# A fused adaLN attention block: the last two x tiles loaded on ScalarE's queue

## The chip, the cores and the metric

The kernel runs on one core of a Trainium2 chip. The metric is the device time of one execution in microseconds, as the median of several runs. Beside it stands one profiled execution of the same kernel, from which all views of the profile come; its span is counted from the first to the last instruction of the program and is a little shorter than the device time.

## The reference

x is 2 x 256 tokens of 1152 features, c is 2 x 1152, all in bfloat16:

```python
B, N, D = (2, 256, 1152)
mod = (_silu(c) @ w_mod).reshape(B, 6, 1, D)
shift_a, scale_a, gate_a, shift_m, scale_m, gate_m = [mod[:, i] for i in range(6)]
h = _layernorm(x, axis=-1) * (1 + scale_a) + shift_a
qkv = h @ wqkv
q, k, v = (qkv[..., :D].copy(), qkv[..., D:2 * D].copy(), qkv[..., 2 * D:].copy())
p = _softmax(jnp.einsum('bqd,bkd->bqk', q, k) * D ** (-0.5), axis=-1)
a = jnp.einsum('bqk,bkd->bqd', p, v) @ wo
return x + gate_a * a
```

Only the first three of the six modulation vectors (shift, scale, gate) reach the output.

## The kernel before, in words

**Tiles.** The 512 tokens are four tiles of 128 (`x_sb[:, t, :]`, 288 KB each, tiles 0 and 1 of the first batch entry, 2 and 3 of the second). The 1152 features are nine blocks of 128 (`KT`). Weights are loaded in pieces: `wS` holds the scale columns of `w_mod`, `wH` the shift columns, `wG` the gate columns, `wK` the key columns of `wqkv`, `wqv` the chunks of the query and value columns, `wO` the output projection. All of them, 21 MB, pass through SyncE's DMA queue in the order in which the code issues them; only c, and one of the last pieces of the output, are issued on ScalarE's queue.

**Order.** Every engine's instructions are recorded by a thin wrapper (`spq` for SyncE, `sca` for ScalarE, `vec`, `ten`, `gps`) and at the end `pin` fixes the order on each engine to the order in the code. A DMA that is issued through `sca` thus stands in ScalarE's instruction stream at the place where the code has it, and what is behind it on ScalarE is issued after it. Since every operation passes through one wrapper, nearly all of them have the same line (L78) in the profile and are told apart by their tiles.

The transfers take eight DMA semaphores in turn, in the order of the code over both queues. Before a transfer is issued, its queue waits until the transfer that had the same semaphore before, eight places earlier, has landed. So at most eight transfers are under way at once.

**The early stage, where the change lies.** The fillers are 13 matmuls on a constant that keep TensorE busy until the first real work. Meanwhile:

- c arrives, `sca.activation(out=e_sb, ... Exp)` and three VectorE steps make silu(c) in `scT_f`; ScalarE spreads it in `silu_rep` to `scT_rep`.
- Tile 1 gets its mean and variance on VectorE (`dve_stats`, `dve_aggr`) and is centred there (`centre`). For tiles 0, 3 and 2 the mean comes from ScalarE: `act_mean(t)` is a copy with row sums and then a small scaling of the sums to the mean. `centre(t)` then subtracts it on VectorE.
- TensorE turns the centred tiles by `turned` (nine 128 x 128 transposes into a PSUM bank `tp`), VectorE copies the first three blocks out of it to `xnT` and ScalarE the rest (`from_psum`).
- TensorE makes the first three blocks of the scale (`scale_A`, into `psS` and `psSA`), VectorE multiplies the turned tile with it (`scaled`, into `hTs`), and TensorE starts the keys (`k_part`, into six accumulators `acc`, and `early_half`, into `psE`), for tiles 0 and 1 together, then tile 3, then tile 2.
- The second third of the scale (`psM`) is made between the transposes of tile 2 and its `k_part`.

The six accumulators take the six PSUM banks of one pool, which held the fillers and the transposes of tiles 0 and 1; an accumulator can only start when the copy out of the bank before it is done. The transposes of tiles 3 and 2 follow each other in one other bank.

ScalarE's order in this stage is: issue of c, exponential, `act_mean(0)`, `silu_rep`, `act_mean(3)`, copy of tile 0's transposes, `act_var(0)`, `act_mean(2)`, copy of tile 3's transposes, copy of `psE`, copy of tile 2's transposes, `act_var(2)`. `act_var` is a square with row sums for the variance. SyncE's order is: x tiles 1, 0, 3, five pieces of `wS`, three pieces of `wK`, x tile 2, the next piece of `wK`, three pieces of `wS`, three of `wK` and so on.

After this stage come the rest of the keys, the queries, the scores, the softmax, the values and the output projection; none of their lines is touched.

```python
def act_mean(t):
    sca.activation(out=xc[:, t, :], in_=x_sb[:, t, :], func=ACT.Copy, accum_out=sums[:, t, 0:1])
    sca.activation(out=mv[:, t, 0:1], in_=sums[:, t, 0:1], func=ACT.Copy, scale=1.0 / D)
```

Of the kernel before, what the change touches and what calls it, by code (L numbers as in the profile page):

```python
# [16 lines left out]
def kernel(  # L17
# [10 lines left out]
    P = 128  # L28
# [17 lines left out]
    x_f = x.rearrange("b n d -> (b n) d")  # L46
# [39 lines left out]
    sca = _Rec(nc.scalar, act_seq)  # L86
    ten = _Rec(nc.tensor, pe_seq)
    spq = _Rec(nc.sync, sp_seq)
# [11 lines left out]
    def tok(b):  # L100
# [5 lines left out]
        out=ident, in_=ident, compare_op=ALU.not_equal, fill=1.0, base=0,  # L106
# [14 lines left out]
        out=pick, in_=pick, compare_op=ALU.is_ge, fill=0.0, base=0,  # L121
# [3 lines left out]
        out=pick, in_=pick, compare_op=ALU.is_ge, fill=0.0, base=NT - 1,  # L125
# [6 lines left out]
    x_sb = act.tile([P, TT, D], BF16)  # L132
# [6 lines left out]
    wS = wmpool.tile([P, KT, D], BF16, tag="wS")  # L139
    wH = wmpool.tile([P, KT, D], BF16, tag="wH")  # L140

    def load_x(t):
        spq.dma_start(out=x_sb[:, t, :], in_=x_f[t * P : (t + 1) * P, :])

    def load_mod(tile_, which, k0, k1, c0, c1):
        spq.dma_start(out=tile_[:, k0:k1, c0:c1], in_=wmod_v[:, k0:k1, which, c0:c1])
# [1 line left out]
    def load_k(k0, k1, c0=0, c1=D):  # L148
        spq.dma_start(out=wK[:, k0:k1, c0:c1], in_=wqkv_v[:, k0:k1, D + c0 : D + c1])

    PAIRS = ((0, 2), (2, 4), (4, 6), (6, 8), (8, 9))
    CA = KA * P
    load_x(1)
    load_x(0)
    load_x(3)
    for k0, k1 in PAIRS:
        load_mod(wS, 1, k0, k1, 0, CA)
    load_k(0, 1, 0, CA)
    load_k(0, 1, CA, WE)
    load_k(1, 2, 0, WE)  # L160
    load_x(2)
    load_k(2, 3, 0, WE)
    CM = KM * P
    for k0 in range(0, KT, 3):
# [20 lines left out]
    fillers(13)  # L185
    e_sb = small.tile([P, 2 * KT], F32, tag="e_sb")
    sca.activation(out=e_sb, in_=cT, func=ACT.Exp, scale=-1.0)
    scT_f = const.tile([P, KT, B], F32)
    scT_rep = const.tile([P, KT, NR // B, B], BF16)

# [10 lines left out]
    def silu_rep():  # L201
        sca.copy(out=scT_rep, in_=scT_f.unsqueeze(2).to_broadcast([P, KT, NR // B, B]))
# [25 lines left out]
# [3 lines that stand above are left out]
# [140 lines left out]
    centre(0)  # L371
    silu_rep()
    act_mean(3)

    def bank(name="tp", n=KT - KA, pool=psum, tag="mm"):
        return pool.tile([P, n, P], BF16, tag=tag, name=name)
# [342 lines left out]
```

## Time and profile before

| what | value |
|---|---|
| median of 3 runs | 97.02 us (96.97 to 97.61) |
| the profiled execution | 97.0 us, span 95.2 us |
| granted TensorE clock | 1.0 |
| TensorE busy | 90.8 us (95%) |
| VectorE busy | 70.6 us (74%) |
| ScalarE busy | 33.5 us (35%) |
| HBM read, written | 19.76 MB, 1.18 MB |
| DMA share in 6.8 to 14.9 us | 1.01, 344 GB/s |

The profile names engines PE (TensorE's matmuls), PEld (its weight loads), DVE (VectorE), ACT (ScalarE), POOL (GpSimd) and SP (SyncE). ACTq and SPq are the instruction queues of ScalarE and SyncE, in which DMAs are issued. A row of a timeline has the start in us, the length, the engine, the operation, the tiles it writes and reads, how many of them were merged, and in brackets how long the engine was idle before it and what released it. The mean length of a matmul is not its cost, because matmuls overlap; in the chain of waits their ends are taken apart.

### The profile page before, as it was taken

The page shows a single profiled execution, that of the slowest core. Times are in us where ns is not written, and L with a number is a line of the kernel's source. Part 1 is how long each engine was busy: PE and PEld are TensorE (multiplying, and loading weights), DVE is VectorE, ACT ScalarE, POOL GpSimd, SP SyncE. Part 2 cuts the span into 40 slices and gives each one's busy share as a digit, 9 for nine tenths or more (in the row PEclk, how much of TensorE's full clock was granted, in tenths as well). Part 3 has the DMA queues.
Part 4 walks back from the last instruction along what each step waited for, and adds up shares of the span by engine and source line. Part 5 has one row for each costly group of instructions (what it writes and reads, how often), then busy time and mean ns, then how long its engine had stood idle before and what let it go on. Part 6 is the DMA issues. An engine that isn't in the chain of part 4 may idle for free.

```text
span 95.2 us, 1731 instructions
## 1 busy us (share of the span) xinstructions
PE 90.8 (95%) x678; PEld 54.6 (57%) x682; DVE 70.6 (74%) x138; ACT 33.5 (35%) x68; POOL 21.4 (22%) x26
## 2 busy tenths in 40 slices
PE   5998999999999999999999999999999999999980
PEld 1338899454436444444458665665668756656670
DVE  0488689134998999999997999990129577998880
ACT  5069867201571935322340455242225400000020
POOL 6600000810000000000000000009999980025000
PEclk9999999999999999999999999999999999999999
DMA  2999999999999999999999802200000000303131
GB/s 76 299 336 337 313 361 384 386 392 405 395 379 399 380 402 410 375 376 361 372 406 410 342 39 55 60 2 0 0 0 0 0 0 7 124 0 124 75 117 56
DMA packets 19015, 21.31 MB, mean 224 GB/s; under 512 B 2752, under 2 KB 13632, under 8 KB 19008
## 3 DMA queue, kind: packets, MB, share of 16 engines
q1 hardware_dynamic: 18592, 21.16, 62.2%
q10 hardware_dynamic: 416, 0.05, 0.4%
q8 instruction: 5, 0.08, 0.3%
q14 instruction: 2, 0.02, 0.0%
HBM read 19.76 MB, written 1.18 MB: 220 GB/s over the span
## 4 chain that ended last, share of the span: by engine, by line
PE 95%; DVE 1%; issue 0%; ACT 0%
PE ps L78 64%; PE acc L78 13%; PE junk_ps L78 6%; PE s_ps L78 4%; PE tp L78 2%; PE psE L78 1%; PE psH L78 1%; PE psL L78 1%; PE psM L78 1%; PE psSA L78 1%; PE psS L78 0%; PE spread_ps L78 0%; DVE hTs L78 0%; ACT o_sb L78 0%; DVE junk_rhs L78 0%
## 5 line engine op out<-in xcount | busy, mean ns | idle before, releaser
L78 POOL PARTITION_ALL_REDUCE gate_bc<-gacc x2 | 13.7, 6887 | 44.8 <-DVE gacc L78 44.8
L78 DVE SCALAR_TENSOR_TENSOR gacc<-wG,scT_f,gacc 128x1152 f32<-128x1152 bf16 x16 | 22.7, 1418 | 0.5
L78 PE MATMUL ps<-wqv,hT 128*128 128x384 bf16 x108 | 17.7, 326 | 0.0
L78 PE MATMUL ps<-hT,wqv 128*128 128x512 bf16 x80 | 17.6, 379 | 0.1
L78 PE MATMUL ps<-wO,attnT 128*128 128x384 bf16 (+1 forms) x108 | 17.0, 319 | 0.0
L78 PEld LDWEIGHTS <-attnT 128*128 128x128 bf16 x126 | 11.4, 98 | 6.3
L78 PEld LDWEIGHTS <-hT 128*128 128x128 bf16 x108 | 10.6, 98 | 6.9
L78 PEld LDWEIGHTS <-wK 128*128 128x128 bf16 x123 | 10.1, 97 | 6.9 <-issue 0.5
L78 PE MATMUL acc<-hTs,wK 128*128 128x128 bf16 (+2 forms) x88 | 13.2, 292 | 0.5 <-DVE hTs L78 0.3
L78 PEld LDWEIGHTS <-wqv 128*128 128x128 bf16 x81 | 7.9, 98 | 9.5
L78 ACT CAST qkT<-ps 128x512 bf16<-128x512 f32 x10 | 5.7, 584 | 10.8 <-PE ps L78 10.8
L78 DVE TENSOR_TENSOR ga<-ps,gate_bc 128x384 f32<-128x384 f32 (+1 forms) x12 | 6.5, 538 | 2.7 <-PE ps L78 2.7
L78 ACT CAST v_sb<-ps 128x384 bf16<-128x384 f32 x10 | 4.7, 477 | 9.8 <-PE ps L78 9.8
L78 DVE TENSOR_TENSOR o_sb<-ga,x_sb 128x384 bf16<-128x384 f32 (+1 forms) x12 | 6.8, 564 | 0.4
L78 PE MATMUL junk_ps<-junk_rhs 128*128 128x512 bf16 x13 | 5.7, 630 | 1.1 <-DVE junk_rhs L78 1.1
L78 DVE TENSOR_TENSOR xnT<-xnT,rstd_bc 128x512 bf16<-128x512 bf16 x9 | 5.5, 684 | 1.6 <-ACT rstd_bc L78 1.6
L78 ACT CAST o_sb<-ps 128x128 bf16<-128x128 f32 (+1 forms) x2 | 0.5, 240 | 17.0 <-PE ps L78 17.0
L78 DVE BATCH_NORM_STATS2 stats<-x_sb 128x6 f32<-128x384 bf16 x6 | 3.1, 552 | 2.7 <-DMA x_sb<-in_x_dram 2.7
L78 PE MATMUL ps<-hTs,wK 128*128 128x512 bf16 x20 | 4.8, 380 | 0.1
L78 DVE CAST attnT<-ps 128x512 bf16<-128x512 f32 (+1 forms) x6 | 3.5, 603 | 1.7 <-PE ps L78 1.7
L78 DVE CAST v_sb<-ps 128x384 bf16<-128x384 f32 x2 | 1.1, 558 | 4.6 <-PE ps L78 4.6
L78 DVE TENSOR_SCALAR hTs<-xnT,s1p 128x256 bf16<-128x256 bf16 (+1 forms) x20 | 4.2, 272 | 0.1
(82 smaller groups left out, 88.0 us busy)
## 6 DMA issues: line engine op xcount, KB each, us to landing
wqv<-in_wqkv_dram SPq DMA_DIRECT2D x5, 864.0 KB, 10.1
wG<-in_w_mod_dram SPq DMA_DIRECT2D x3, 864.0 KB, 9.7
wO<-in_wo_dram SPq DMA_DIRECT2D x3, 864.0 KB, 8.5
wH<-in_w_mod_dram SPq DMA_DIRECT2D x4, 576.0 KB, 7.2
wS<-in_w_mod_dram SPq DMA_DIRECT2D x6, 288.0 KB, 6.4
wK<-in_wqkv_dram SPq DMA_DIRECT2D x6, 288.0 KB, 7.2
x_sb<-in_x_dram SPq DMA_DIRECT2D x4, 288.0 KB, 4.2
wqv<-in_wqkv_dram SPq DMA_DIRECT2D x3, 288.0 KB, 8.4
```

The lines of the kernel that those rows point to most:

```text
L78: r = fn(*a, **k)
```

## The change

`load_x` gets the queue as an argument. The load of x tile 3 moves from the third place of SyncE's queue to ScalarE's queue, behind the exponential of silu, and that of x tile 2 from between two pieces of `wK` on SyncE's queue to ScalarE's queue, behind `act_mean(3)`. The order of everything else stays, on all engines. On ScalarE the two issues are two more instructions; on SyncE there are two fewer.

```diff
-    def load_x(t):
-        spq.dma_start(out=x_sb[:, t, :], in_=x_f[t * P : (t + 1) * P, :])
+    def load_x(t, eng=spq):
+        eng.dma_start(out=x_sb[:, t, :], in_=x_f[t * P : (t + 1) * P, :])
...
     load_x(1)
     load_x(0)
-    load_x(3)
     for k0, k1 in PAIRS:
         load_mod(wS, 1, k0, k1, 0, CA)
     load_k(0, 1, 0, CA)
     load_k(0, 1, CA, WE)
     load_k(1, 2, 0, WE)
-    load_x(2)
     load_k(2, 3, 0, WE)
...
     sca.activation(out=e_sb, in_=cT, func=ACT.Exp, scale=-1.0)
+    load_x(3, sca)
...
     silu_rep()
     act_mean(3)
+    load_x(2, sca)
```

In the semaphores' turn, tile 3 now comes behind the fourth piece of `wS` and tile 2 behind the first of the next three pieces of `wS`. So the second of these three waits for tile 3 to land, and the third of the last three pieces of `wS` for tile 2; tile 2 itself waits for the fourth piece of `wS`.

## The prediction

> **What bounds the kernel now.** I read the page's busy row first, then the chain of waits in order of time, then ScalarE's and VectorE's timelines between 3 and 16 us, then the DMA issues one by one. The busy row and one wait list say how much there is to win at all:
>
> ```profile
> PE 90.8 (95%) x678; PEld 54.6 (57%) x682; DVE 70.6 (74%) x138; ACT 33.5 (35%) x68; POOL 21.4 (22%) x26
> ```
>
> The list of TensorE's own waits between 6 and 26 us has this one line:
>
> ```profile
> PE acc L78 <- DVE hTs L78: 0.3, 1, 0.3
> ```
>
> TensorE is the bound. It starts at 1.11 us on fillers that last to 6.81 whatever is loaded, and from there to 92.5 its work is nearly back to back. Its gaps are 0.33 us ahead of the first K product (9.33), about 0.12 us ahead of the third K step (11.52 to 11.64, where its weight load waits for wK) and some 0.15 us at 14.7 to 14.9. So nothing done to loads can bring more than about 0.6 us, 0.6% of the time. A loss has no such limit: whatever comes late to TensorE before 26 us is added to the end, since no later gap takes it up. The chain of waits shows the last of these places, the x tile 2 part (columns: start, length, what):
>
> ```profile
> 13.69 0.45 PE tp L78 x8
> 14.14 0.71 PE psM L78 x27
> 14.85 0.03 issue
> 14.88 1.17 PE acc L78 x18
> ```
>
> The 1.17 us are `k_part` for tile 2. What it waits for comes from x tile 2 through ScalarE (row sums and mean) and VectorE. ScalarE's timeline (start, length, idle before and its releaser in brackets):
>
> ```profile
> 3.90 0.22 ACT L78 ACTIVATE e_sb<-c_sb 128x18 f32<-128x18 bf16 x1 [1.84 <-DMA c_sb<-in_c_dram]
> ...
> 7.34 1.16 ACT L78 ACTIVATE xc<-x_sb 128x1152 bf16<-128x1152 bf16 x1
> ...
> 8.62 0.20 ACT L78 ACTIVATE mv<-sums 128x1 f32<-128x1 f32 x1
> 8.73 0.78 ACT L78 COPY xnT<-tp 128x768 bf16<-128x768 bf16 x1
> ...
> 10.99 1.16 ACT L78 ACTIVATE xc<-x_sb 128x1152 bf16<-128x1152 bf16 x1 [0.32 <-DMA x_sb<-in_x_dram]
> ...
> 12.28 0.20 ACT L78 ACTIVATE mv<-sums 128x1 f32<-128x1 f32 x1
> ```
>
> The row at 10.99 is the key one: ScalarE already waits 0.32 us there for x tile 2 to land. VectorE goes on from its mean (12.28):
>
> ```profile
> 12.51 0.52 DVE L78 TENSOR_SCALAR xc<-x_sb,mv 128x1152 bf16<-128x1152 bf16 x1
> 12.95 1.02 DVE L78 BATCH_NORM_STATS2 stats<-x_sb 128x6 f32<-128x384 bf16 x2
> 14.18 0.36 DVE L78 COPY xnT<-tp 128x384 bf16<-128x384 bf16 x1 [0.21 <-PE tp L78]
> 14.57 0.58 DVE L78 TENSOR_SCALAR hTs<-xnT,s1p 128x128 bf16<-128x128 bf16 x3
> ```
>
> Centring of tile 2, two statistics of tile 3, the copy of the transposes, the three scalings, then the products at 14.88. This string has one slack, the 0.21 us ahead of the copy. **A microsecond of delay of tile 2 costs TensorE 0.8 us.**
>
> The DMA issues give latencies. In order, with issue times from SyncE's and ScalarE's timelines: x tile 1 (0.79), tile 0 (1.25), tile 3 (1.71), tile 2 (6.85), and c on ScalarE's queue (0.81); the last number is us from issue to landing:
>
> ```profile
> x_sb<-in_x_dram SPq DMA_DIRECT2D x1, 288.0 KB, 2.9
> ...
> x_sb<-in_x_dram SPq DMA_DIRECT2D x1, 288.0 KB, 4.2
> ...
> x_sb<-in_x_dram SPq DMA_DIRECT2D x1, 288.0 KB, 4.6
> ...
> x_sb<-in_x_dram SPq DMA_DIRECT2D x1, 288.0 KB, 4.1
> ...
> c_sb<-in_c_dram ACTq DMA_DIRECT2D x1, 4.5 KB, 3.1
> ```
>
> Tile 1 went into an empty system: 2.9 us. The others stand in SyncE's first-in first-out backlog. From 2 us to 52 us the DMA row of the page is at 9, so whatever is put ahead pushes the rest back.
>
> **The change, part by part.** The two loads keep size and shape; they only change queue and time of issue. Nothing is added to VectorE or TensorE.
>
> *Tile 3, issue moved from 1.71 on SyncE to behind the exponential on ScalarE.* The exponential runs at 3.90, released by c, so the issue falls at about 4.0. ScalarE's issue of c lasted 0.46 us, the nearest row; here it ends at 4.5 while ScalarE waits for tile 0 until 5.46, so it costs nothing. Landing: 4.0 plus 2.9 to 3.1 (tile 1, and c on this queue) is 6.9 to 7.1; with 4.6 (tile 3's own latency in the backlog) 8.6. Its user, the row sums at 7.34, is held until 7.34 by the scT_rep copy in any case. I take 7.1: free. At 8.6 the row sums would start 1.3 us late, and the ScalarE copy of tile 0's transposes (8.73 to 9.51) with them; that copy frees the bank of the sixth accumulator, which TensorE takes at 9.87, so 1.3 + 0.36 of issue less the 0.36 of cover is 1.3 us of stall.
>
> *What tile 3's removal does on SyncE.* The issues behind it move up by 0.46 us until the fifth wS transfer, which waits for tile 1 to land; the next ones wait for older landings too, because the built program takes eight DMA semaphores in turn. The first four wS transfers may land up to 0.85 us earlier (288 KB at the 344 GB/s of the 6.8 to 14.9 us window), but tile 3 is then put among them, and with the DMA engines full the fifth wS lands after the same bytes as before, at 8.7 (issue 4.16, 4.5 us). Bounds: 0 to 0.33 us won at the first K product, minus what follows next. I take 0.
>
> *ScalarE's issue of tile 2.* It stands behind tile 3's mean, so it can't go before that is dispatched; the next instruction started at 8.73, so issue at 8.73 instead of 6.85: 1.9 us later. It holds ScalarE's queue for 0.36 us (the final output's issue) to 0.46 (c): the copy of tile 0 now starts at 9.1 to 9.2, ends at 9.9 to 10.0, and the sixth accumulator stalls TensorE by 0.0 to 0.15 us. That is absorbed by the 0.12 ahead of the third K step, provided its wK (issue 7.38, 4.2 us, 11.6) comes earlier, which it does: tile 2 no longer stands ahead of it on SyncE. ScalarE, free for tile 2's row sums at 10.67 until now (the read of tile 0's square sums ends there), is then ready at 11.05 to 11.15, so 10.99 can't be beaten.
>
> *Tile 2's landing,* the term that decides. It is not behind SyncE's backlog but shares the DMA engines with it. From below, 2.9 us (tile 1, empty system): landing 11.6. From above, 4.1 us (its own old latency): 12.8. Nearest in queue and load is c, 3.1 us, though only 4.5 KB; a full tile takes a little longer, so I take 3.2: landing 11.9 instead of 10.97, row sums 0.94 us later.
>
> The sum: 0.94 of delay less 0.21 of VectorE slack is 0.73 us at tile 2's products. The other ways to that point are no later: the transposes of tile 2 need the mean of tile 2 and ScalarE's copy of tile 3 (12.38 to 13.05, now to 14.0) and would end near 14.7, ahead of the two statistics at 14.9. Behind it TensorE is back to back, so 0.73 reaches the end. Nothing else is won there: the 0.12 and 0.15 us gaps lie ahead of the same wait. The profiled execution took 97.0 us (span 95.2 and 1.8 around it; the median shown is 97.02): 97.0 + 0.7 = **97.7 us**. With 2.9 us of latency it is 0.43, 97.4; if the landing were no later than ScalarE is ready (11.05), about 0, 97.0.
>
> By the Trainium skill (DMA: Bandwidth & Descriptors, Issuing engines are not separate DMA queues) loads from several engines run on the same 16 DMA engines and interleave, and only issue time is saved. No row here shows a big load on ScalarE's queue beside the backlog; the rule speaks against a shorter latency and is the first rival's argument.
>
> **The rivals.**
>
> *Tile 2 wins no latency on the other queue.* The engines are full, so it takes the 4.1 us it took before: landing 8.73 + 4.1 = 12.8, row sums 1.87 us later, less 0.21 is 1.66: 98.7 us. For it: DMA at 9 in every slice. Against it: the 4.1 us were spent mostly behind SyncE's earlier transfers, which a load on another queue need not await. It decides from a latency of 3.45 us on, where the loss passes 1%, 0.97 us.
>
> *Both loads are served in order of arrival over both queues,* so the new queue passes nothing. Tile 3 lands near 8.4, since the four wS of the backlog go ahead; tile 2 is then issued at 9.8 and lands like the wK rows issued then, some 5 us later, near 15: 15.0 - 10.99 - 0.21 = 3.8 us, 100.8 us. For it: c, only 4.5 KB, landed at 3.9, after tile 1's 288 KB at 3.7. Against it: c was issued just after tile 1 anyway, so nothing tells the two orders apart.
>
> The Trainium skill (the same page, Queues, rings and completion order) has each DMA engine go round between the queues it has work for, a packet at a time, which speaks against this rival; no row here decides it.
>
> *The early loads win, and tile 2 lands in time.* With tile 3 and tile 2 out of SyncE's way the fifth wS and the third wK come earlier, and tile 2 needs only 2.3 us because its queue is empty. Then up to 0.33 + 0.12 + 0.15 = 0.6 us is won: 96.4 us. Against it: even tile 1 took 2.9 us in an empty system, and 10.99 can't be beaten on ScalarE; so most of these gaps would remain, at best about 96.9.
>
> **How the numbers follow.** A measurement of this kernel tells about 1% from no change. My forecast (latency 2.9 to 3.4 us, 97.4 to 98.0) has 0.47, tile 2 in time or a gain within 1% 0.10, the first rival (3.45 us to 4.6 us, 98.0 to 99.2) 0.31, order of arrival 0.08, a gain over 1% 0.04, as the gaps do not add up to it. So faster 0.04, same 0.57, slower 0.39. The range is 96.9 to 99.0: it takes in the forecast, the tile that is just in time, and most of the first rival.
>
> **What would show it.** After: the issue of tile 3 on ScalarE at 4.0 and of tile 2 near 8.7; the row sums of tile 3 at 7.34 without a wait for DMA; those of tile 2 near 11.9 with an idle time of some 0.9 us put down to x_sb; VectorE's centring of tile 2 at 13.4; TensorE's tile 2 products at 15.6; the rest shifted by 0.7 us. I am wrong if tile 3 is late at 7.34, if tile 2 lands before 11.2 or after 12.3, or if TensorE has the delay made up before the end.

## The result, and the profile after

The changed kernel takes 102.83 us (median of 6, 102.69 to 103.78) against 97.01 us before: a ratio of 1.061, 95% interval 1.057 to 1.065. The forecast was 97.7 us, in a range of 96.9 to 99.0; the loss is 5.8 us instead of 0.7. The profiled execution took 102.78 us, span 100.8 against 95.2. Here and below a median takes in every execution, and a ratio leaves out those that took over 1.5% longer than the fastest of the same kernel.

The chain of waits of the changed kernel, in order of time (start, length, what), no longer runs through TensorE's early work. It runs through the two moved loads:

```profile
3.98 4.56 DMA x_sb<-in_x_dram
...
8.56 1.26 ACT xc L78 x2
...
9.86 5.89 DMA x_sb<-in_x_dram
...
15.77 1.26 ACT xc L78 x2
...
17.89 1.01 PE tp L78 x8
18.90 1.21 PE psM L78 x27
20.11 1.63 PE acc L78 x18
...
98.12 0.21 ACT o_sb L78
```

In the kernel before, the last row of the chain is

```profile
92.49 0.21 ACT o_sb L78
```

Tile 3 is issued at 3.98 and lands at 8.54. Its row sums keep ScalarE until the mean is dispatched at 9.85, and only then, at 9.86, is tile 2 issued: one load waits for the use of the other. Tile 2 lands at 15.74, 4.8 us later than before. The three TensorE rows from 17.89 are those shown of before (0.45, 0.71 and 1.17 us for the same work); all three have grown too. From 20.11 the chain is TensorE alone up to the last output, as before.

On ScalarE's timeline the waits stand in the brackets:

```profile
8.56 1.16 ACT L78 ACTIVATE xc<-x_sb 128x1152 bf16<-128x1152 bf16 x1 [2.01 <-DMA x_sb<-in_x_dram]
...
10.23 0.80 ACT L78 COPY xnT<-tp 128x768 bf16<-128x768 bf16 x1 [0.18 <-issue]
...
15.77 1.16 ACT L78 ACTIVATE xc<-x_sb 128x1152 bf16<-128x1152 bf16 x1 [3.58 <-DMA x_sb<-in_x_dram]
```

and TensorE's own waits (total, times, longest) name what they became there:

```profile
PE tp L78 <- ACT xnT L78: 3.1, 1, 3.1
PE acc L78 <- ACT xnT L78: 1.4, 1, 1.4
...
PE tp L78 <- DVE xc L78: 1.0, 1, 1.0
```

The 1.4 us are the sixth accumulator, whose bank is freed by the copy at 10.23. The 3.1 us are tile 2's transposes, whose bank is freed by ScalarE's copy of tile 3's, which stands behind tile 2's row sums. So both waits end with ScalarE, which is held by the two loads. The 1.0 us costs nothing: the fillers ended earlier in this execution, and the first transposes start at 6.77 (6.92 before).

The stages after the pause show why the three chain rows grew (columns: stage, its length, busy us and instructions of TensorE, its weight loads, VectorE, ScalarE and GpSimd, granted clock, DMA share, GB/s):

```profile
15.00:17.00 2.00, 0.00 (x0) 0.00 (x0) 0.00 (x0) 1.23 (x2) 0.00 (x0) 1.00 1.03 358
17.00:19.00 2.00, 1.11 (x15) 1.14 (x16) 1.51 (x4) 1.29 (x4) 0.00 (x0) 0.72 0.91 274
19.00:21.00 2.00, 2.00 (x36) 2.00 (x34) 1.83 (x10) 1.67 (x3) 0.00 (x0) 0.50 1.01 325
21.00:23.00 2.00, 2.00 (x20) 1.56 (x19) 0.62 (x4) 0.74 (x3) 1.50 (x4) 0.93 0.85 226
```

After the pause the granted clock is 0.72, then 0.50, before it recovers. **The loss adds up so:** the row sums of tile 2 start 4.78 us later (15.77 against 10.99); the rest, from there to the last ScalarE copy, takes 82.35 us (to 98.12) against 81.50 (to 92.49), 0.85 more. Together 5.63 us, which is the difference of the two chains' ends.

### The profile page after: what moved, and what is told of

Same layout as the page of the kernel before. It is cut to its first block, busy times and chain, and to the rows that moved or that the text cites. A ratio compares the mean times of both kernels' runs of the same rounds, so it can differ in the third digit from the quotient of the medians.

```text
span 100.8 us, 1735 instructions
## 1 busy us (share of the span) xinstructions
PE 91.1 (90%) x682; PEld 55.8 (55%) x682; DVE 70.9 (70%) x138; ACT 33.7 (33%) x68; POOL 21.4 (21%) x26
## 4 chain that ended last, share of the span: by engine, by line
PE 80%; DMA 13%; ACT 4%; issue 0%
PE ps L78 61%; DMA x_sb<-in_x_dram 10%; PE acc L78 10%; PE s_ps L78 4%; DMA c_sb<-in_c_dram 3%; ACT xc L78 3%; PE psH L78 1%; PE psM L78 1%; PE tp L78 1%; PE psL L78 1%; PE psE L78 1%; ACT xnT L78 1%; PE spread_ps L78 0%; ACT o_sb L78 0%; ACT mv L78 0%
## 5 line engine op out<-in xcount | busy, mean ns | idle before, releaser
L78 PE MATMUL acc<-hTs,wK 128*128 128x128 bf16 (+2 forms) x90 | 14.1, 306 | 1.7 <-ACT xnT L78 1.4
L78 PEld LDWEIGHTS <-wK 128*128 128x128 bf16 x123 | 10.8, 103 | 8.1 <-issue 2.0
L78 ACT CAST qkT<-ps 128x512 bf16<-128x512 f32 x10 | 5.7, 584 | 10.8 <-PE ps L78 10.8
L78 PE MATMUL tp<-ident,xc 128*128 128x128 bf16 x36 | 3.2, 239 | 4.1 <-ACT xnT L78 3.1
L78 PE MATMUL junk_ps<-junk_rhs 128*128 128x512 bf16 x13 | 4.5, 521 | 1.1 <-DVE junk_rhs L78 1.1
L78 ACT ACTIVATE xc<-x_sb 128x1152 bf16<-128x1152 bf16 x3 | 3.5, 1163 | 6.0 <-DMA x_sb<-in_x_dram 6.0
L78 DVE COPY xnT<-tp 128x384 bf16<-128x384 bf16 (+2 forms) x7 | 2.2, 347 | 4.1 <-PE tp L78 4.1
L78 PEld LDWEIGHTS <-xc 128*128 128x128 bf16 x36 | 2.5, 107 | 4.6 <-DVE xc L78 4.4
```

The source lines that it names most:

```text
L78: r = fn(*a, **k)
```

## The experiments

Two theories. **A**: a transfer is served in the order of its arrival over both queues, so that a load on ScalarE's queue passes nothing that SyncE has issued before it; what counts is the time of issue. **B**: ScalarE's queue has a share of the DMA engines of its own, but is slow to start. The edits are shown against the changed kernel, except for the small load and for tile 3 behind c, which are shown against the kernel before. Landings and waits are those of the one profiled execution of each run.

**Tile 3 alone** (tile 2 back on SyncE):

```diff
     load_k(1, 2, 0, WE)
+    load_x(2)
...
     act_mean(3)
-    load_x(2, sca)
```

> Only the load of x tile 3 is moved (ScalarE's queue, behind the exponential); tile 2 stays on SyncE between the wK pieces. Theory A (a load is served in order of arrival over both queues, so tile 3 issued at 4.0 lands behind the five wS pieces at 8.5): tile 3's row sums start at 8.5 instead of 7.34, the copy of tile 0's transposes ends near 10.7, the sixth accumulator starts near 10.8 instead of 9.87; tile 2 lands before 11.2 but ScalarE is ready for it only at 11.9, so its row sums are 0.9 late; no long TensorE pause, clock 1.0: 97.7 us (97.4 to 98.1). Theory B (a load issued on ScalarE's queue shares the engines with SyncE's queue but is itself slow to start): the same for this kernel, since tile 3's latency is the 4.6 us already seen. It sizes the tile 3 part of the 5.8 us.

Median 98.1 us, ratio 1.011 (1.008 to 1.014). In the profiled execution, the longest of the five (99.82 us, at a clock of 0.983; the others took 97.84 to 98.36), tile 3 was issued at 4.00 and landed 4.9 us later, its row sums started at 8.95, the sixth accumulator at 11.18 after a wait of 1.2 us, and tile 2's row sums at 12.18, without a wait for its load. So the tile 3 part by itself is about 1.1 us where the clock stays up. Both theories had the same forecast here.

**Tile 2 alone** (tile 3 back in third place on SyncE):

```diff
     sca.activation(out=e_sb, in_=cT, func=ACT.Exp, scale=-1.0)
-    load_x(3, sca)
```

> Only the load of x tile 2 is moved (ScalarE's queue, behind tile 3's mean); tile 3 stays third on SyncE. It is issued at 8.7. Theory A (order of arrival): it lands after the transfers that SyncE has issued by 8.7, near 13.8 to 14.4, row sums near 14.0, 3 us late; TensorE pauses some 2.5 us before tile 2's transposes, perhaps with some cycles of a lower clock behind it: 99.9 us, up to 100.5. Theory B (slow start of 1.9 to 2.7 us on ScalarE's queue, then a share of its own): first packets at 10.6 to 11.4, landing 12.2 to 13.0: 98.0 to 98.8. My prediction's 3.2 us of latency: 97.7.

Issued at 8.22, landed 5.6 us later at 13.84, between those of the two `wS` pieces that SyncE had issued at 8.43 (14.95) and 7.43 (11.96); the one issued at 8.01 landed at 14.16. This lies in A's range and not in B's 12.2 to 13.0, but the order is not strictly that of arrival: tile 2 landed 0.3 us before the piece issued 0.2 us ahead of it. TensorE waited 2.5 us before tile 2's transposes. The four executions fall into two groups by granted clock: 97.9 and 99.17 us at 1.0, 100.66 and 101.14 (the profiled one) at 0.98, with the lower clock behind the pause; the ratio of 1.016 (1.010 to 1.023) compares the first group alone and does not say whether the loss reaches 2%. A's 99.9 to 100.5 us fits neither group, and where tile 2 landed in the first group is not on record.

**Tile 2 on ScalarE's queue, but early:**

```diff
     silu_rep()
+    load_x(2, sca)
     act_mean(3)
-    load_x(2, sca)
```

(and tile 3 third on SyncE).

> Tile 3 stays third on SyncE; tile 2 is on ScalarE's queue, but behind the copy that makes scT_rep, so that it is issued at 6.9, when SyncE issued it in the kernel before. Theory A (the queue doesn't matter, the time of issue does): lands near 11.0 as before, 97.0 us within 0.3. Theory B (ScalarE's queue is slow to start): first packets 0.9 to 1.6 us later than from SyncE, landing 11.9 to 12.6, 97.7 to 98.4 us.

97.58 us, 1.007 (1.004 to 1.010). A missed the time, and B came near it for a wrong reason. The `scT_rep` copy, and with it the issue, came at 5.95 instead of 6.9, because tile 0 landed 0.8 us earlier in this execution. Tile 2 then landed at 9.95, 4.0 us after its issue; with 0.9 us of slow start added to the old 4.1, B gives 10.95 at the earliest. It took the place of a `wK` piece, for which TensorE waited:

```profile
PE acc L78 <- DMA wK<-in_wqkv_dram: 0.8, 1, 0.8
```

The landing speaks for A.

**Both on SyncE, at the places where they were served:**

```diff
     for k0, k1 in PAIRS:
         load_mod(wS, 1, k0, k1, 0, CA)
+    load_x(3)
...
     for k in range(KA, KM):
         load_k(k, k + 1)
+        if k == KA:
+            load_x(2)
```

> Neither load is on ScalarE's queue. Tile 3 stands on SyncE behind the fifth wS piece (issue near 4.2), tile 2 behind the first 1152-column piece of wK (issue near 9.9): the places between SyncE's transfers at which they were served in the changed kernel. Theory A: tile 3 lands near 8.5, tile 2 near 15.5, 102.5 us (0.3 less than 102.8 for ScalarE's issue that is gone). Theory B: without ScalarE's slow queue both land some 1 us earlier, 100.5 to 101.5 us.

101.72 us, 1.045 (1.039 to 1.050), with no load of x on ScalarE at all. In its list of DMA issues, tile 2 (issued at 8.77):

```profile
x_sb<-in_x_dram SPq DMA_DIRECT2D x1, 288.0 KB, 6.2
```

and in that of the changed kernel the `wK` piece that SyncE issued at 9.51, and tile 2, issued at 9.86 on ScalarE:

```profile
wK<-in_wqkv_dram SPq DMA_DIRECT2D x1, 288.0 KB, 5.5
x_sb<-in_x_dram ACTq DMA_DIRECT2D x1, 288.0 KB, 5.9
```

On SyncE's own queue the load takes as long as on ScalarE's. The time is 1.1 us below the changed kernel's and 0.8 below what A gave; it is nearer to B's range, and it is the latencies that speak against B. Tile 2 was issued 1.1 us earlier than in the changed kernel (8.77 against 9.86) and landed 0.8 us earlier (14.98): SyncE waits for tile 3's landing (8.37), by the semaphores' turn, but not for its mean. The execution at a clock of 1.0 took 100.44 us, the three at 0.98 took 101.68 to 102.07.

**A small load in tile 2's place.** One more load of c in the kernel before:

```diff
     act_mean(3)
+    sca.dma_start(out=c_probe, in_=c.rearrange("b (p k) -> p b k", p=P))
```

> The kernel before, with one more load of c, 4.5 KB, into a tile that nobody reads, on ScalarE's queue behind tile 3's mean, issued at 8.3 to 8.7: the place of tile 2's load, without its 288 KB. Theory A (order of arrival): it lands with the transfers that SyncE issued just before, 5 us later, near 13.5. Theory B (a share of its own for ScalarE's queue, only slow to start): 2 to 3 us after its issue, near 11.5. The time stays at 97.0 to 97.3 us in both: the issue holds ScalarE for 0.35 us, which the bank of the sixth accumulator takes up.

Issued at 7.67 on ScalarE. Its row, and that of the `wK` piece which SyncE issued at 7.81:

```profile
wK<-in_wqkv_dram SPq DMA_DIRECT2D x1, 256.0 KB, 4.0
c_probe<-in_c_dram ACTq DMA_DIRECT2D x1, 4.5 KB, 4.3
```

4.5 KB take as long as 256 KB: both land at 11.8 to 12.0, the small load last, although it was issued first. B's 2 to 3 us is excluded. (A's 5 us was for a later issue.) The time rose to 97.4 us, 1.004 (1.001 to 1.008).

What the 4.3 us are, the record of the DMA packets tells for the stretch from 9.2 to 11.5 us (q1 is SyncE's queue, q10 ScalarE's; then packets, MB and their share of the 16 DMA engines' time):

```profile
q1 hardware_dynamic: 485, 0.66, 88.4%
q10 hardware_dynamic: 272, 0.00, 6.6%
```

All 272 packets of the small load lie in this stretch. They are 6.6% of 2.3 us, some 0.15 us of work for each engine, but they run from 1.5 us after the issue to 3.8 us after it, side by side with SyncE's. So the load did not simply wait for what was issued before and then pass in one piece.

**Tile 3 on ScalarE right behind c:**

```diff
     load_x(0)
+    load_x(3, sca)
```

(before the exponential; tile 3's load on SyncE is gone, tile 2 in its old place there).

> Tile 3 alone is on ScalarE's queue, issued right behind c at 1.3 us, a little before SyncE would issue it; tile 2 is in its old place on SyncE. Theory A (the queue doesn't matter, the time of issue does): tile 3 lands near 6.3, in time for 7.34, 97.0 us within 0.4. Theory B (a load on ScalarE's queue starts 1 to 1.6 us later than one on SyncE's): it lands near 7.5 to 8, row sums 0.2 to 0.7 late, 97.2 to 97.6 us.

97.22 us, 1.002 (0.999 to 1.005): no difference. Issued at 1.30, landed 4.1 us later at 5.43, row sums at 6.57; A had given a landing near 6.3, B 7.5 to 8. The other queue is harmless when the issue is early.

**Tile 2 one step up in the changed kernel** (ahead of `act_mean(3)`):

```diff
     silu_rep()
+    load_x(2, sca)
     act_mean(3)
-    load_x(2, sca)
```

> The changed kernel with tile 2's load one step up in ScalarE's queue: behind the copy that makes scT_rep, ahead of tile 3's row sums; tile 3 still behind the exponential. Theory A: tile 2 is issued at 6.0 and lands near 10 to 10.5, before ScalarE is ready for it (11.9, because tile 3 is as late as before); TensorE loses the tile 3 part alone: 98.0 us (97.7 to 98.5), no lower clock in most executions. Rival: two big loads on ScalarE's queue cost by themselves, whatever the place: over 100 us.

Five of ten executions, at a clock of 1.0, took 97.36 to 98.15 us, ratio 1.008 (1.003 to 1.013); four, at 0.983, took 100.0 to 100.5, as long as the rival gave, and the profiled one, at 0.997, took 99.17. The median of all ten is 98.66. One line of code thus takes back some 5 us of the 5.8 where the clock stays up, and 4.2 by the median. In the profiled one tile 2, issued at 6.32, landed at 12.4, later than the 10.5 expected: 6.1 us of latency, like the 6.3 of the `wK` piece which SyncE issued beside it at 5.88. In the packet record nearly all of tile 2's 144 packets had started by 10.9 us; the last six started one by one from 11.14 to 11.92, so a small rest of the load set its landing. Why that rest was late is open.

**The pause kept warm:** 24 matmuls of zero weights in TensorE's pause of the changed kernel.

```diff
+    for _ in range(24):
+        ten.matmul(accs[0][:, tok(0)], lhsT=zero_w, rhs=hTs[:, 0, tok(0)],
+                   start=False, stop=False, skip_group_check=True)
     centre(2)
```

> The changed kernel with 24 matmuls of zero weights, 256 columns each, added to the first accumulator (it gains nothing but zeros) ahead of tile 2's transposes; they take about 2.6 of the 3.1 us that TensorE pauses there. Theory A (arrival order makes tile 2 late by 4.8 us, of which 4.6 reach TensorE, and the pause then lowers the granted clock for some 4 us, which costs another 1.1): clock 1.0 throughout, 101.7 us (101.4 to 102.1). Rival: the lower clock lies beside other waits and costs nothing: 102.8 us.

102.17 us, 1.050 (1.043 to 1.058), at a clock of 1.0 in all four executions; the expected range ended at 102.1. In the profiled one, tile 2 landed 0.7 us later than in the changed kernel's (16.42), and the chain from there is:

```profile
16.42 0.02 issue
16.44 1.26 ACT xc L78 x2
...
20.02 1.17 PE acc L78 x18
...
97.55 0.21 ACT o_sb L78
```

The `k_part` of tile 2 takes 1.17 us again instead of 1.63. From the row sums to the last copy it is 81.11 us (97.55 - 16.44), against 82.35 in the changed kernel: 1.24 us is the price of the clock, by one execution of each. The median moved by only 0.7, and the two ratios' intervals just touch (1.057 and 1.058). In the profiled execution the later landing of tile 2 accounts for this; for the others it is not shown. So filling the pause kept the clock up; what that is worth is 0.7 us by the medians and 1.2 by the chain.

## Why the prediction was wrong

**The bound was read rightly.** TensorE's early gaps left at most 0.6 us to win, no run here was faster than the kernel before, and a delay behind 14.9 went to the end in full. The string from tile 2's row sums to its products also held: 4.78 us late, less the slack ahead of them (81.50 - 81.11 = 0.39, where the text took 0.21), plus 1.24 for the clock, is 5.63. (This sum closes by construction, since its terms come from the chains that it explains; what it shows is the size of each.) One reading did not hold: the fillers do not last to 6.81 "whatever is loaded". They took 4.50 us and ended at 5.60 in the changed kernel's profile, against 5.70 us before; why is not shown, and it did not set the time.

**The step that failed is tile 2's landing.** The text gave it 3.2 us from issue, between tile 1's 2.9 and its own old 4.1, and took c's 3.1 us on ScalarE's queue as the nearest row. It was 5.9. The landing came 3.8 us after the forecast one (15.74 against 11.9): 2.7 by the latency, 1.1 by the later issue. c's row was misread: it was issued at 0.81, when only one x tile was ahead of it, so it measured an almost empty system and not the queue. The probe of the same size took 4.3 us beside more transfers. Nor was the old 4.1 us an upper bound: it belongs to the backlog at 6.85, and SyncE's transfers issued near 9.5 to 10 took 5.5 and more, before and after. The rows for that were in the trace of before; these are the pieces that SyncE issued at 8.42 and 9.91, on both sides of tile 2's new issue:

```profile
wS<-in_w_mod_dram SPq DMA_DIRECT2D x1, 288.0 KB, 5.2
...
wK<-in_wqkv_dram SPq DMA_DIRECT2D x1, 288.0 KB, 6.0
```

**Tile 3 was not free.** 7.1 was taken for its landing, 8.6 was written as the other end with 1.3 us of stall; it landed at 8.54, and the stall was 1.4. That end was not carried on: tile 3's lateness also moves tile 2's issue, from 8.73 to 9.86. The two terms were bounded one by one, but they follow each other on ScalarE's queue.

**A rival was right in what counts.** Order of arrival over both queues, with a chance of 0.08, gave tile 3 at 8.4, tile 2's issue at 9.8 and its landing near 15, 100.8 us. Measured: 8.54, 9.86, 15.74. The 2.0 us that it still lacks are 0.7 of landing and 1.24 of clock, which no rival had. It was right that the new queue brings no shorter latency and that the two latencies stand in series. That the service is strictly in order of arrival is more than the runs show: the order of landing was broken by 0.3 us with tile 2 alone and by 0.1 us with the small load. The text said that nothing told the two orders apart, and gave the rival little all the same.

The Trainium skill (DMA: Bandwidth & Descriptors, Issuing engines are not separate DMA queues) says that issuing from another engine saves only sequencer time. The latencies here agree: 5.9 us on ScalarE's queue at 9.86, 6.2 us on SyncE's at 8.77. What the same page has on going round between the queues by packets (Queues, rings and completion order) was cited against the right rival. The packet record agrees with it in part. With tile 2 alone, its 144 packets ran between 10.8 and 13.6 us beside 763 of SyncE's, and by an estimate from the packets' starts and ends (162 pairs in which SyncE's packet starts 3 or 4 ns before the other's end, less 64 that chance gives) some 100 of them are followed on the same engine by one of SyncE's; if each of the 16 engines had passed its part in one piece, it would be 16. But going round brought no earlier landing: 4.5 KB took 4.3 us.

SyncE's third late `wS` piece, which takes its semaphore turn behind tile 2, was issued at 15.76, after 3.4 us of waiting. TensorE's chain has no wait for it, so it didn't set the end here; that was read from the chain and not tried by itself.

## What to carry to other kernels

A load on another engine's queue gained nothing on the backlog here: when the DMA engines are full, count its latency from its time of issue and from what the main queue's transfers issued at that time take, not from a row in an empty system. A load that stands behind another load's use has both latencies in series, so bounds of such terms are added, not taken one by one. If a load has to be early, move its issue up; on which queue it stands is second.

## What was not expected of the hardware

The pause in front of tile 2's transposes, 3.1 us, cost up to 1.24 us more, by a granted clock of 0.72 and 0.50 in the 4 us after it; all six executions of the changed kernel had a mean clock of 0.966 to 0.983, and all with the pause filled had 1.0. Shorter pauses did it too, but not each time: in the profiled execution with tile 3 alone, TensorE had three pauses of 0.9, 0.3 and 1.2 us between 5.8 and 11.2, and then

```profile
11.00:13.00 2.00, 1.82 (x9) 1.31 (x9) 0.46 (x1) 2.00 (x4) 0.19 (x1) 0.54 1.06 312
13.00:15.00 2.00, 2.00 (x17) 1.73 (x15) 0.82 (x4) 1.09 (x4) 0.00 (x0) 0.60 0.94 282
```

a clock of 0.54 and 0.60, while its other four executions kept 0.997 to 1.0. The profiled execution with tile 2 one step up had pauses of 1.4, 0.3, 0.8 and 0.8 us, and its clock stayed at 1.00 in every stretch of 2 us from 5 to 23. So the length of the pauses alone does not tell whether the clock drops. The Trainium skill (TensorE: Matmul & The Clock Gate, Part 1: The HAM clock gate) puts the drop after an idle window of about 3.4 us; in the execution with tile 3 alone, pauses of 1.2 us and less in a row were enough.
